# A decode block with a streamed key/value cache: from a framework that unrolls every step to hand-placed waits and hardware loops on two engines

## The chip, the core and the metric

The kernel runs on one core of a Trainium2 chip. The core has five instruction streams: TensorE (PE in the profile, with weight loads as PEld), VectorE (DVE), ScalarE (ACT), GpSimd (POOL) and SyncE (SP), and 16 DMA engines that carry all traffic from and to HBM. The metric is the device time of one execution in microseconds; less is better. The kernel before was timed three times: 1318.71, 1318.73 and 1319.01 us, a median of 1318.73.

## The reference

One token for each of two batch entries goes through attention over a long cache and is gated by a small feed-forward block. All data are float32.

```
xn = layernorm(x)                         # x: [2, 1, 512]
q  = xn @ wq                              # wq: [512, 4096] -> 32 heads of 128
k, v                                      # caches: [2, 8, 32768, 128]; 4 query heads share one
p  = softmax(q . k * 128**-0.5)           # over 32768 tokens
s  = concat(p @ v) @ wo                   # wo: [4096, 512]
g  = silu((relu_gate(xn @ W_gate) * (xn @ W_up)) @ W_down)    # 512 -> 1792 -> 512
out = x + s * g
```

`relu_gate(a)` is `a * (a > 0)`. The two caches are 268 MB each and are read once; the weights are 28 MB.

## The kernel before

**Tiles and steps.** There are 16 groups (batch entry b, key/value head hk), taken as g -> (g % 2, g // 2), with 32768 tokens each. A step handles TK = 8192 tokens of K, a 4 MB load with 64 tokens on each of 128 partitions. A group has NU = 4 steps, so there are NK = 64 steps s, and V runs four steps behind K: step s makes the scores of tile s and, at odd s, multiplies the tiles s - 5 and s - 4 with V. Four more steps (64 to 68) drain this.

**One step.** VectorE turns the K tile in four parts of 128x2048 (`k_transpose`, L336; the last step has its tokens in another order, L339, all others L344) into tiles named `kts`, drawn from a pool of five buffers (`ktpool`, L58). TensorE multiplies them with the query: 16 matmuls on four column groups (`scores`, L350), the first four of them one per part, then eight, and in the last four one per part again. VectorE takes the scores out of PSUM with their maximum (`take_scores`, L366). At a group's end (`tile_maximum`, L381, `maximum`, L387) the maximum over the tiles is turned, spread and negated, and ScalarE takes the exponentials of four tiles. A step later TensorE arranges a tile's weights (`weights`, L411), VectorE transposes them in 32x32 blocks (`take_weights`, L421), and `values` (L424) multiplies with V, 16 matmuls a tile. `sums`, `take_o` and `finish_group` (L440 to L484) divide by the sum, pick the head's own rows and put them, turned by VectorE, into the tile `ots`. At the end `project_near` and `project_far` (L488, L507) multiply `ots` with wo in eight parts, and the result is gated, added to x and stored.

**Loads.** All loads are issued by SyncE in one queue, in the order of the code (`load`, L135, with its DMA at L136). K goes into a ring of two 4 MB buffers: K of step s + 2 is issued when step s has transposed its tile. V comes as 8 MB for two steps into one wide buffer, which wq, the gate and up weights and the down weights use in turn at the start: V of s - 3 and s - 2 is issued at odd s behind K, when the values before it are done. So from step 3 on the queue holds K, K, V (8 MB) for every two steps. At the end come four parts of wo, the last V in halves, and the last four parts of wo, the last one cut in three (`load_late`, L189).

**Order of the work.** The loop at L577 writes one step after another, all unrolled in Python. A tile framework places buffers and derives every semaphore wait from the reads and writes of tiles; `pin` (L559) keeps the order of the code on TensorE and VectorE. In step s the order is: first transposed part; scores of s - 1 taken out; group output; maximum; second and third part; `finish_group`; `weights`; fourth part and `scores(s)`; `take_weights`; `values` at odd s.

## Time and profile before

| | |
|---|---|
| median of three runs | 1318.73 us |
| span of the profiled execution | 1316.7 us |
| instructions in the span | 10568 |
| busy TensorE, matmuls | 894.2 us (68%) |
| busy VectorE | 694.2 us (53%) |
| busy ScalarE | 51.3 us (4%) |
| HBM read | 564.67 MB, 429 GB/s over the span |

The profiled execution has only its span, from its first to its last instruction; what lies around the span is part of the timed 1318.73 us, so that the two stand 2.0 us apart. In the rows of the page, a group of instructions is given as line, engine, operation, tile written <- tiles read, shape and count, then busy time and mean duration, then the idle time of its engine just before them with what ended it. A window row gives a stretch of time, its length, the busy time of PE, PEld, DVE, ACT and POOL with instruction counts, TensorE's granted clock, the mean share of the 16 DMA engines that was busy, and GB/s. The queue rows give a queue, its kind, packets, MB and share of the 16 engines. In SP's timeline a row of two DMAs spans both issues; waits between them are inside.

### The profile page before, as it was taken

How to read it: one execution, taken by the hardware profiler on the slowest of the kernel's cores; microseconds unless marked ns; L12 is line 12 of the kernel's file. 1: busy time of each engine (PE TensorE's matmuls, PEld its weight loads, DVE VectorE, ACT ScalarE, POOL GpSimd, SP SyncE). 2: the span in 40 equal slices, each digit the busy share in tenths (PEclk: the TensorE clock that was granted, in tenths of full speed). 3: DMA queues.
4: the chain of work that ended last, by engine and by line, in shares of the span. 5: the costliest groups of instructions: out<-in, count | busy, mean ns of one | idle time of the engine just before them, and what ended most of it. 6: DMA issues, size and time to landing. Idle time of an engine off the chain costs nothing.

```text
span 1316.7 us, 10568 instructions
## 1 busy us (share of the span) xinstructions
PE 894.2 (68%) x4700; PEld 211.3 (16%) x4700; DVE 694.2 (53%) x627; ACT 51.3 (4%) x133; POOL 0.7 (0%) x6
## 2 busy tenths in 40 slices
PE   3766767576776767766676757766676675676775
PEld 1221111111111111111111111111121111111111
DVE  3676664454665545566454566544466654546611
ACT  0000000000000000000000000000000000000000
POOL 0000000000000000000000000000000000000000
PEclk9777788798788788888888988878878887987798
DMA  9999999999999999999999999999999999999997
GB/s 407 436 429 431 433 450 427 433 424 434 437 438 435 427 432 433 433 430 439 435 442 419 432 432 440 438 433 426 430 436 433 436 436 437 425 432 432 438 423 318
DMA packets 16353, 565.35 MB, mean 429 GB/s; under 512 B 1826, under 2 KB 1842, under 8 KB 2228
## 3 DMA queue, kind: packets, MB, share of 16 engines
q1 hardware_dynamic: 16280, 564.67, 99.3%
q8 instruction: 37, 0.61, 0.2%
q14 instruction: 8, 0.07, 0.0%
q10 hardware_dynamic: 28, 0.01, 0.0%
HBM read 564.67 MB, written 0.00 MB: 429 GB/s over the span
## 4 chain that ended last, share of the span: by engine, by line
DMA 71%; DVE 26%; PE 2%; issue 0%; DVEq 0%; SPq 0%
DMA k<-in_A_k_cache_dram 65%; DVE kts L344 22%; DMA wo_late<-in_A_wo_dram 2%; DMA wo<-in_A_wo_dram 2%; DMA wq<-in_A_wq_dram 2%; DVE sc L371 1%; DVE os L451 1%; PE pq L231 1%; PE s L357 1%; PE pr L399 1%; DVE kts L339 1%; DVE ob L479 0%; DVE mrow L396 0%; DVE nb L403 0%; DVE ots L484 0%
## 5 line engine op out<-in xcount | busy, mean ns | idle before, releaser
L344 DVE STREAM_TRANSPOSE kts<-k 128x2048 f32<-128x2048 f32 x252 | 567.9, 2286 | 482.4 <-DMA k<-in_A_k_cache_dram 482.4
L357 PE MATMUL s<-kts,qt 128*32 128x512 f32 x2048 | 482.4, 714 | 193.5 <-DVE kts L344 191.0
L429 PE MATMUL o_ps<-v,sc 128*16 128x512 f32 x2048 | 256.8, 652 | 81.5 <-DMA v<-in_A_v_cache_dram 81.4
L357 PEld LDWEIGHTS s<-kts,qt 128*32 128x32 f32 x2048 | 91.4, 126 | 585.1 <-DVE kts L344 318.5
L429 PEld LDWEIGHTS o_ps<-v,sc 128*16 128x16 f32 x2048 | 58.1, 103 | 263.4 <-issue 163.6
L407 ACT ACTIVATE sc<-sc,nb 128x512 f32<-128x512 f32 x64 | 45.4, 710 | 1125.1 <-DVE nb L403 1125.1
L413 PE MATMUL pt<-sc,perm 128*128 128x512 f32 x128 | 82.8, 735 | 1.2 <-ACT sc L407 1.1
L371 DVE TENSOR_SCALAR_CACHE_REDUCE sc<-s 128x512 f32<-128x512 f32 x64 | 43.0, 672 | 47.0 <-PE s L357 47.0
L385 PE MATMUL pr<-ident,m 128*1 128x128 f32 x16 | 5.6, 347 | 80.0 <-DVE m L383 80.0
L422 DVE STREAM_TRANSPOSE sc<-pt 128x512 f32<-128x512 f32 x64 | 43.3, 677 | 19.7 <-PE pt L413 19.6
L413 PEld LDWEIGHTS pt<-sc,perm 128*128 128x128 f32 x128 | 23.9, 217 | 57.3 <-issue 44.6
L399 PE MATMUL pr<-negone,mrow 1*128 1x1 f32 x32 | 9.1, 351 | 33.1 <-DVE mrow L396 33.1
L467 PE MATMUL po<-os,heads 128*128 128x512 f32 x32 | 31.3, 1079 | 0.0
L451 DVE SCALAR_TENSOR_TENSOR os<-o_ps,rl,own 128x512 f32<-128x512 f32 x16 | 12.0, 750 | 11.5 <-PE o_ps L429 10.0
L385 PEld LDWEIGHTS pr<-ident,m 128*1 128x1 f32 x16 | 1.3, 79 | 94.7 <-DVE m L383 89.5
L399 PEld LDWEIGHTS pr<-negone,mrow 1*128 1x128 f32 x32 | 7.7, 298 | 37.4 <-DVE mrow L396 37.4
L231 PE MATMUL pq<-wq,xt 128*32 128x512 f32 x64 | 9.3, 744 | 6.0 <-DMA wq<-in_A_wq_dram 6.0
L449 DVE RECIPROCAL rl<-pl 128x1 f32<-128x1 f32 x16 | 2.6, 164 | 17.8 <-PE pl L444 17.8
L407 ACT ACTIVATION_READ_ACCUMULATOR sc<-sc,nb 128x1 f32 x64 | 11.9, 187 | 0.0
L223 PE MATMUL px<-ident,boot 32*128 32x32 f32 x4 | 0.7, 300 | 16.1 <-DVE boot L217 16.1
L339 DVE STREAM_TRANSPOSE kts<-k 128x2048 f32<-128x2048 f32 x4 | 9.0, 2280 | 0.0
L242 DVE COPY qs<-pq 128x512 f32<-128x512 f32 x2 | 1.4, 692 | 14.3 <-PE pq L231 14.3
(79 smaller groups left out, 109.5 us busy)
## 6 DMA issues: line engine op xcount, KB each, us to landing
k<-in_A_k_cache_dram SPq DMA_DIRECT2D x64, 4096.0 KB, 27.0
v<-in_A_v_cache_dram SPq DMA_DIRECT2D x3, 4096.0 KB, 25.6
wo<-in_A_wo_dram SPq DMA_DIRECT2D x4, 1024.0 KB
v<-in_A_v_cache_dram SPq DMA_DIRECT2D x2, 2048.0 KB
wgu<-in_B_W_gate_dram SPq DMA_DIRECT2D x1, 3584.0 KB, 19.6
wgu<-in_B_W_up_dram SPq DMA_DIRECT2D x1, 3584.0 KB
wd<-in_B_W_down_dram SPq DMA_DIRECT2D x1, 3584.0 KB
wo_late<-in_A_wo_dram SPq DMA_DIRECT2D x3, 1024.0 KB, 31.9
```

Source lines behind the costliest of these rows:

```text
L231: nc.tensor.matmul(pq[half][32 * c : 32 * c + 32, :], xn[:, k, :], wqt[:, k, half, c * 512 : (c + 1) * 512], start=(k == 0), stop=(k == NK ...
L339: nc.vector.transpose(part.rearrange("p (h r) e k -> p h (r e k)", h=2), in_halves(KT[t])[:, :, c].rearrange("p h r d -> p h (r d)"),)
L344: nc.vector.transpose(part.rearrange("p r e k -> p (r e k)"), KT[t][:, c].rearrange("p r d -> p (r d)"),)
L357: nc.tensor.matmul(ps[Q * c : Q * c + Q, :], qt[:, b, hk, e, :], kts[c][:, :, e, :], start=(e == 0), stop=(e == 3),)
L371: nc.vector.tensor_scalar(ST[t].rearrange("p r m -> p (r m)"), SPS.pop(t), SCALE, None, op0=ALU.mult, op1=ALU.max, accum_out=MX[g][:, u : ...
L399: nc.tensor.matmul(pr[:, 256:257], mrow.rearrange("o c k h -> o (c k h)"), negone, start=True, stop=True)
L407: nc.scalar.activation(st, st, AF.Exp, bias=nbias, scale=1.0, accum_out=LS[g][:, u : u + 1])
L413: nc.tensor.matmul(PW[t], perm.rearrange("p k c h -> p (k c h)"), ST[t].rearrange("p r m -> p (r m)"), start=True, stop=True,)
L422: nc.vector.transpose(ST[t].rearrange("p r m -> p (r m)"), PW.pop(t))
L429: nc.tensor.matmul(ops[g % 2][a : a + NC * REP, :, :], w[:, r, : NC * REP], v[:, r // 8, :, r % 8, :] if t == NK - 1 else v[:, :, r, :], s ...
L451: nc.vector.scalar_tensor_tensor(OS[g], ops[g % 2], rl, own.unsqueeze(2).to_broadcast([P, NC, DH]), op0=ALU.mult, op1=ALU.mult,)
L467: nc.tensor.matmul(po, heads[:, b].rearrange("p h m -> p (h m)"), o.rearrange("p c d -> p (c d)"), start=(b == 0), stop=(b == B - 1), skip ...
```

## The change

The kernel is written again without the tile framework. What it computes, the loads, their order and the order of steps stay. In detail:

- Buffers are placed by hand. The turned K parts have four fixed tiles, one per part, instead of five in rotation. K has two slots, V the wide buffer, scores, weights, outputs and the small products two PSUM banks each.
- Each operation is recorded with keys that it reads and writes. A class works out which semaphore values it must wait for (one counter for each engine, one semaphore for each load stream) and leaves out what is known already.
- TensorE and VectorE run steps 0 to 7 as straight code, then steps 8 to 63 as a loop of seven passes of eight steps, then steps 64 to 68. In the loop, each awaited value stands in a register that is raised by additions. SyncE, ScalarE and GpSimd stay unrolled.
- All tiles have the order of tokens that only the last step had, so that each pass has the same addresses.
- The turned head outputs, whose place depends on the head, go to a fixed tile on VectorE, and ScalarE copies them to their place. The query of a group is copied by GpSimd into one of two fixed tiles.
- The projection of q is done one half after the other. The frame is a block of engine programs; at the end GpSimd clears the semaphores.

The core of the diff; the class that works out the waits and the set-up code are left out, since they write the same operations in another form:

```diff
+PERIOD = 8
+    def looped(self, engine, first, last):
+        rounds = (last - first) // PERIOD
...
+        for same in zip(*bodies):
+            waits = {}
+            for s in sorted({s for o in same for s in o.waits}):
+                v = max(o.waits[s] - n * stride[s] for n, o in enumerate(same) if s in o.waits)
...
+    def emit(self, engine, eng, sems, loop=None):
...
+        with eng.Fori(0, rounds):
+            for o, waits in body:
+                for s, v in sorted(waits.items(), key=lambda w: w[0] == engine):
+                    if not stride[s]:
+                        eng.wait_ge(sems[s], v)
+                        continue
+                    if v != at[s]:
+                        eng.reg_add(regs[s], regs[s], v - at[s])
+                        at[s] = v
+                    eng.wait_ge(sems[s], regs[s])
+                run(o)
+            for s, r in regs.items():
+                eng.reg_add(r, r, start[s] + stride[s] - at[s])
...
-    ktpool = ctx.enter_context(tc.tile_pool(name="ktpool", bufs=5))
+    kts = [sbuf(f"kts{c}", P, NR * P, align=ALIGN) for c in range(NC)]
...
     def k_transpose(t, c):
-        part = ktpool.tile([P, NR, 4, Q], F32, tag="kt", align_bytes=ALIGN, name=f"kts_{t}_{c}")
-        if t == NK - 1:
...
+        src = kslot[t % 2]
+        dve(
+            lambda e: e.transpose(
+                kts[c].rearrange("p (h n) -> p h n", h=2),
+                in_halves(src)[:, :, c].rearrange("p h r d -> p h (r d)"),
+            ),
+            [f"k{t % 2}"],
+            [f"kts{c}"],
+        )
...
+        for c in range(NC):
+            pe(one(0, c), [f"kts{c}", f"qcur{b}"], [f"s{t % 2}"])
+        pe(chain([one(e, c) for e in (1, 2) for c in range(NC)]), [f"qcur{b}"], [f"s{t % 2}"])
+        for c in range(NC):
+            pe(one(3, c), [f"kts{c}", f"qcur{b}"], [f"s{t % 2}"])
...
+    def take_query(g):
+        b, hk = group(g)
+        pg.op(
+            "POOL" if g >= 2 else "DVE",
+            lambda e: e.tensor_copy(qcur[b], qt[:, b, hk]),
+            ["qt"],
+            [f"qcur{b}"],
+        )
...
-        nc.vector.transpose(ots[:, hk].rearrange("p j m -> p (j m)"), ob)
+        dve(
+            lambda e: e.transpose(ot, ob),
+            ["ob"],
+            ["ot"],
+        )
+        act(
+            lambda e: e.copy(ots[:, hk].rearrange("p j m -> p (j m)"), ot),
+            ["ot"],
+            [f"ots{hk}"],
+        )
...
+    sems = {s: nc.alloc_semaphore(f"sem_{s}") for s in pg.count}
+    with nc.Block(no_gpsimd_drain=True) as block:
...
+        @block.vector
+        def _(e):
+            pg.emit("DVE", e, sems, loop=(PERIOD, NK))
+
+        @block.tensor
+        def _(e):
+            pg.emit("PE", e, sems, loop=(PERIOD, NK))
+
+    nums = sorted(s.num for s in sems.values())
+    nc.gpsimd.sem_clear(range(nums[0], nums[-1] + 1))
```

## The prediction, made before the changed kernel ran

> **What bounds the kernel now.** I read the page's first three parts first, then the busy time by windows, at last the timeline of one pair of steps. Span, load stream and queues:

> ```profile
> span 1316.7 us, 10568 instructions
> PE 894.2 (68%) x4700; PEld 211.3 (16%) x4700; DVE 694.2 (53%) x627; ACT 51.3 (4%) x133; POOL 0.7 (0%) x6
> DMA  9999999999999999999999999999999999999997
> q1 hardware_dynamic: 16280, 564.67, 99.3%
> q8 instruction: 37, 0.61, 0.2%
> q14 instruction: 8, 0.07, 0.0%
> 700.00:1000.00 300.00, 205.61 (x1051) 46.94 (x1050) 159.10 (x138) 11.72 (x32) 0.00 (x0) 0.84 1.00 433
> ```

> The 16 DMA engines carry the loads (q1) for 99.3% of the span; the last two columns of the windows row say share 1.00 at 433 GB/s, with TensorE (PE) busy 205.6 and VectorE (DVE) 159.1 of 300 us. Bytes set the time, and the change moves none of the 564.67 MB. What is left is how the stream starts, how it ends, and what else the same engines carry. That is q8 and q14, packets of instructions: 0.61 MB / 37 = 16 KB and 0.07 MB / 8, some 8 KB. The program has 4700 matmuls and 4700 weight loads; 0.61 MB / 9400 is 65 bytes for each, so q8 brings PE's instructions, 254 to a packet, and an 8 KB packet holds about 128. The end of the stream, by windows (second number from the right: share of 16 engines):

> ```profile
> 1304.00:1305.00 1.00, 1.00 (x12) 0.06 (x4) 0.00 (x0) 0.00 (x0) 0.00 (x0) 0.50 1.00 408
> 1305.00:1306.00 1.00, 1.00 (x8) 0.37 (x8) 0.13 (x1) 0.00 (x0) 0.00 (x0) 0.50 0.70 289
> 1306.00:1308.00 2.00, 2.00 (x10) 0.30 (x2) 0.62 (x1) 0.00 (x0) 0.00 (x0) 0.70 0.57 241
> 1308.00:1309.00 1.00, 1.00 (x10) 0.16 (x8) 0.48 (x1) 0.00 (x0) 0.00 (x0) 1.00 0.55 229
> 1309.00:1310.00 1.00, 0.48 (x8) 0.00 (x0) 0.53 (x2) 0.00 (x0) 0.00 (x0) 1.00 0.50 203
> 1310.00:1311.00 1.00, 0.76 (x8) 0.16 (x8) 0.00 (x0) 0.00 (x0) 0.00 (x0) 1.00 0.45 176
> 1311.00:1312.00 1.00, 0.70 (x20) 0.41 (x16) 0.62 (x1) 0.00 (x0) 0.00 (x0) 1.00 0.24 94
> 1312.00:1312.50 0.50, 0.50 (x27) 0.38 (x16) 0.07 (x1) 0.00 (x0) 0.00 (x0) 1.00 0.08 29
> ```

> Share times 16 is the number of engines still loading: 16 until 1305, then 9, 8 from 1309, 4 from 1311, none after 1312.2. Seven engines finish at about 1305.3 (in that second 0.30 x 16 = 4.8 engine-us are missing, 0.7 for each of seven), one at 1308.8, four at 1310.8, four at 1312.2. All have equal bytes, so nine were held up: by 3.5, 5.5 and 6.9 us. I read this as the instruction packets: dealt in turn to eight engines, 36 packets make five on four of them and four on the other four (the 37th may come after the data). 6.9 / 5 = 1.38 and 5.5 / 4 = 1.38: both steps give the same **toll of 1.38 us per 16 KB packet**. The ninth engine, 3.5 us late, would hold VectorE's packets (627 instructions and some 60 waits, 5 to 6 packets: 0.58 each; between 3.5 / 8 = 0.44 and half of 1.38). The chain behind the last byte:

> ```profile
> 1302.96 2.85 PE L429 MATMUL o_ps<-v,sc 128*16 128x512 f32 x16 [2.07 <-DMA v<-in_A_v_cache_dram]
> 1309.25 0.31 DVE L484 STREAM_TRANSPOSE ots<-ob 128x128 f32<-128x128 f32 x1
> 1311.61 0.64 PE L516 MATMUL py<-wo_late,ots 128*32 128x128 f32 x16 [0.30 <-DMA wo_late<-in_A_wo_dram]
> 1312.37 0.82 PE L516 MATMUL py<-wo_late,ots 128*32 128x128 f32 x16
> 1313.90 0.65 SPq L624 DMA_DIRECT2D out_dram<-gy  x1
> ```

> Each load counts as landed with its slowest engine, and the last rows of wo end the kernel: what the worst engine loses to packets, the kernel loses.

> **The change, part by part.** *The loops.* Rows for one period of eight steps:

> ```profile
> L357 PE MATMUL s<-kts,qt 128*32 128x512 f32 x2048 | 482.4, 714 | 193.5 <-DVE kts L344 191.0 <-DVE kts L339 2.5
> L429 PE MATMUL o_ps<-v,sc 128*16 128x512 f32 x2048 | 256.8, 652 | 81.5 <-DMA v<-in_A_v_cache_dram 81.4
> L413 PE MATMUL pt<-sc,perm 128*128 128x512 f32 x128 | 82.8, 735 | 1.2 <-ACT sc L407 1.1
> ```

> By 64 steps that is 32 + 32 + 2 matmuls a step and as many weight loads, 132; eight steps 1056, two group ends 14 each: 1084. From `emit` I count some 57 waits with as many register additions and ten instructions of the loop, so about 1210, 4.8 packets. A matmul of the code is two matmuls and two weight loads in the trace (2048 at L357 for 64 x 16), so the straight steps 0 to 7 are 512 for scores, 16 and 256 for weights and values, 184 for q, 352 for the gated block, ten for a group end and some 60 waits: 1390 (5.5 packets). Steps 64 to 68 are 16 and 256, 192 for wo and some 26 more: 490 (1.9). If a pass finds its instructions still in place, PE loads 5.5 + 4.8 + 1.9, with one ahead at the loop's end 13 packets in place of 37: at most two on an engine, 2.8 us in place of 6.9. VectorE's body is 72 instructions (nine per step with group ends), 51 waits, 51 additions and eight of the loop: 182, 1.4 packets; all told some 430 instead of 690, 3 to 4 packets, 2.3 us on its engine, less than 2.8. Gain: 6.9 - 2.8 = **4.1 us**. If each pass loads its body anew, PE loads 5.5 + 7 x 4.8 + 1.9 = 41, up to 55 when every pass adds a cut packet and one past the end: six or seven on the worst engine, 8.3 to 9.7 us, a loss of 1.4 to 2.8. VectorE then loads 12 + 7 to 14, 19 to 26 packets, all on one engine: 19 x 0.58 = 11.0 to 15.1 us, a loss of 4.1 to 8.2. Nothing in this trace loops, so the trace can't say which; both ends stay in the range. I take the first: the staircase fits packets that go to eight places in turn, and 1210 instructions fill five or six of eight.

> [...]

> *The waits and edges of the loop.* A pass's jump may stall an engine, by how much nothing here shows; what hides it is in one pair of steps:

> ```profile
> 642.13 2.31 DVE L344 STREAM_TRANSPOSE kts<-k 128x2048 f32<-128x2048 f32 x1 [16.86 <-DMA k<-in_A_k_cache_dram]
> 652.84 5.32 PE L357 MATMUL s<-kts,qt 128*32 128x512 f32 x32
> 653.83 12.03 SPq L136 DMA_DIRECT2D k<-in_A_k_cache_dram  x2
> 654.32 2.27 DVE L344 STREAM_TRANSPOSE kts<-k 128x2048 f32<-128x2048 f32 x1
> 671.06 7.06 PE L429 MATMUL o_ps<-v,sc 128*16 128x512 f32 x64 [0.23 <-DMA v<-in_A_v_cache_dram]
> 678.18 0.33 SPq L136 DMA_DIRECT2D v<-in_A_v_cache_dram  x1
> 680.78 2.31 DVE L344 STREAM_TRANSPOSE kts<-k 128x2048 f32<-128x2048 f32 x1 [14.69 <-DMA k<-in_A_k_cache_dram]
> k<-in_A_k_cache_dram SPq DMA_DIRECT2D x64, 4096.0 KB, 27.0
> ```

> A pass ends behind an odd step, where VectorE sits idle for 14.7 us until K lands: a stall up to that costs nothing.

> *Four transposed tiles in place of five.* The first transpose of a step now waits until the scores of the step before have read that tile, ten of the last 13 matmuls. In the odd step above it starts at 654.32 while scores run 652.84 to 658.16; it would start near 657, 2.7 us later, and with it the three transposes, the scores and the issue of K, which leaves SyncE (SP) behind them. A K load takes 27.0 us from issue to landing, its own 4.19 MB at 433 GB/s 9.7 of them: 17 us of other loads lie ahead of it, on the engines ahead of the rest some 5 less. 2.7 comes out of that. The V load waits for the values, and these for V's landing at 671, later than the moved scores: nothing. The tightest place lies in the straight steps:

> ```profile
> 79.45 13.19 SPq L136 DMA_DIRECT2D k<-in_A_k_cache_dram  x2
> 79.48 3.62 PE L357 MATMUL s<-kts,qt 128*32 128x512 f32 x26 [0.61 <-DVE kts L344]
> 79.58 2.31 DVE L344 STREAM_TRANSPOSE kts<-k 128x2048 f32<-128x2048 f32 x1 [0.15 <-DMA k<-in_A_k_cache_dram]
> 0.74 0.40 SPq L136 DMA_DIRECT2D wq<-in_A_wq_dram  x1
> ```

> The second K issue of the first row, K of step 5, ends at 92.6 and begins some 0.3 before. Ahead of it lie wq 8.39 MB, five K of 4.19 and three weights of 3.67, 40.4 MB, or 93.2 us of a stream that was issued at 0.74: gone 94.0 us in, with the same way from issue to first byte. The transpose waits until 79.48 + 3.62 x 10 / 13 = 82.3 instead of 79.58, so the issue moves from 92.3 to 95.0, and an engine without lag runs dry for 1 us, once; an engine with a packet behind it, 1.4 us late, does not. I take nothing and keep 0 to 1.

> *The rest.*

> ```profile
> L344 DVE STREAM_TRANSPOSE kts<-k 128x2048 f32<-128x2048 f32 x252 | 567.9, 2286 | 482.4 <-DMA k<-in_A_k_cache_dram 482.4
> L339 DVE STREAM_TRANSPOSE kts<-k 128x2048 f32<-128x2048 f32 x4 | 9.0, 2280 | 0.0
> L333 ACT ACTIVATE gy<-ps_d 128x128 f32<-128x128 f32 x1 | 0.3, 277 | 76.8 <-PE ps_d L326 76.8
> SPq L136 <- DMA v<-in_A_v_cache_dram: 207.0, 33, 9.3
> ```

> One order of tokens keeps shapes and counts: L339, which has that order now, takes 2280 ns, L344 2286; nothing. ScalarE's copy of the turned head outputs is on the path only in the last group: ots at 1309.56, needed at 1311.61, 2.05 us of cover for about 0.3 (the activation at L333 is nearest, 277 ns) and a hop. If that cover went, 0.4 us of loss. GpSimd's copy of a group's query has four steps to finish. SyncE still issues wq first, 0.74 us in, and its waits for earlier loads that share a semaphore (207.0 us in 33 waits for V) go; the stream is full, so nothing. The frame around the program stays a barrier at either end, within 0.4 us both ways.

> Sum: 4.1 us less. The profiled execution has a span of 1316.7; the median is 1318.73, 2.0 beside it, taken as unchanged. 1318.7 - 4.1 = **1314.6 us**, a profile span of 1312.6.

> **The rivals.** [...]

> *Half the gain, or none*: VectorE's body stays and PE's does not, 1320.1 to 1321.5; or a part of PE's is reloaded, about 30 packets, four on an engine, 5.5 in place of 6.9: 1317.3. Either is within 0.2%.

> *The stream runs dry*: if waits on registers delay the odd steps by over some 10 us, each us more is paid in each of some 28 pairs in the loop; 1 us gives 1347. Against it: the idle 14.7 us, and PE's 205.6 of 300.

> *The loop does nothing*, should it be unrolled again when built: 37 packets as now, 1318.7. I put it with the second.

> **How the numbers follow.** Forecast 0.50; half or none 0.14; loaded anew 0.30; dry 0.06. 0.2% is 2.6 us, about what a measurement of this kernel can tell from no change. So faster 0.50, same 0.14, slower 0.36. Forecast alone: one to three packets on the worst engine, 1313.2 to 1316.0. The range reaches from there through the second case and the larger part of the third, to 1325.0; above it lie the end of the third case (0.08) and the dry one.

> **What would show it.** Right: q8 falls from 37 packets to 12 to 15, the staircase ends within 3 us of its first step, windows in the loop stay at 433 GB/s. [...] A DMA share under 0.98 in windows of 300 us is the dry one. The prediction is wrong at its root if the staircase stays while q8 shrinks: then the packets were not what held the nine engines up.

## The result and the profile after

The changed kernel takes 1315.38 us, the median of nine runs (1314.80 to 1317.09), beside 1318.87 us for the kernel before on the same chip: a ratio of 0.9977, 95% interval 0.9968 to 0.9985. It is 3.5 us faster; 1314.6 us was forecast. The profiled execution is the slowest of the nine, 1317.09 us with a span of 1315.2, so its last microseconds show more than the median has.

The page of the kernel after, first its span, then the load queue and the two queues of instruction packets (packets, MB, share):

```profile
span 1315.2 us, 11033 instructions
...
q1 hardware_dynamic: 16280, 564.67, 99.5%
q8 instruction: 11, 0.18, 0.0%
q14 instruction: 4, 0.03, 0.0%
```

The load is the same to the byte. TensorE's packets (q8) fell from 37 to 11, the packets of 8 KB (q14) from 8 to 4. The same queues of the kernel after, by stretches: 0 to 350 us (TensorE's first pass of the loop ends at about 330), 350 to 1260, and 1260 to 1312:

```profile
q8 instruction: 9, 0.15, 0.1%
...
q1 hardware_dynamic: 10172, 394.33, 100.2%
q14 instruction: 2, 0.02, 0.0%
...
q8 instruction: 2, 0.03, 0.2%
```

Nine of TensorE's packets come while it goes through the straight steps and the first pass, two when it leaves the loop. In the 910 us between, six more passes, there is no row for q8 at all: a pass finds its instructions in place. The two packets of q14 in that stretch move at about 424 and 955 us. One moves at 420 to 424 and one at 952 to 959 us in every kernel of the experiments too, whether VectorE loops or not; so these two belong to an engine that stays unrolled. q14 is not VectorE's alone: of its four packets here the other two, at about 68 and 267 us, are taken as VectorE's.

Windows of the kernel after, one in the loop and then the end of the stream (the last two columns are the DMA share and GB/s):

```profile
700.00:1000.00 300.00, 208.75 (x1054) 51.38 (x1054) 164.13 (x140) 12.32 (x34) 1.17 (x4) 0.82 1.00 434
1304.00:1305.00 1.00, 1.00 (x9) 0.16 (x9) 0.24 (x1) 0.00 (x0) 0.00 (x0) 1.00 0.98 410
1305.00:1306.00 1.00, 1.00 (x2) 0.22 (x2) 0.00 (x0) 0.00 (x0) 0.00 (x0) 1.00 0.96 389
1306.00:1307.00 1.00, 0.67 (x9) 0.16 (x8) 0.88 (x2) 0.00 (x0) 0.00 (x0) 1.00 0.90 356
1307.00:1308.00 1.00, 0.45 (x7) 0.00 (x0) 0.12 (x1) 0.30 (x1) 0.00 (x0) 1.00 0.48 186
1308.00:1309.00 1.00, 0.12 (x4) 0.12 (x8) 0.00 (x0) 0.00 (x0) 0.00 (x0) 1.00 0.12 47
1309.00:1310.00 1.00, 0.94 (x8) 0.03 (x5) 0.00 (x0) 0.00 (x0) 0.00 (x0) 1.00 0.06 25
1310.00:1311.00 1.00, 0.80 (x24) 0.65 (x28) 0.69 (x1) 0.00 (x0) 0.00 (x0) 1.00 0.06 25
```

The loop runs at 434 GB/s, so its waits cost the stream nothing. Two things differ at the end. The long plateau of eight engines at 0.55 is gone: most engines finish between 1306.5 and 1309. But the first step comes later than before: share 0.96 from 1305 to 1306, where it was 0.70. So something holds up even the engines that finish first by more than a microsecond, and in this execution one engine alone (0.06 x 16 = 1) loads on to nearly 1311.

Where that first loss lies is seen in step 3. The timeline of the kernel after, first the K issues of SyncE, then the first transpose of step 3 and the scores that it waits for (the bracket is idle time and what ended it):

```profile
79.41 16.00 SPq L237 DMA_DIRECT2D k<-in_A_k_cache_dram  x2
79.44 3.62 PE L240 MATMUL s<-kts,qcur 128*32 128x512 f32 x26 [0.57 <-DVE kts L648]
82.35 2.31 DVE L648 STREAM_TRANSPOSE kts<-k 128x2048 f32<-128x2048 f32 x1 [2.97 <-PE s L240]
```

The transpose waits for the scores of the step before, 82.35 instead of 79.58, and the second K issue of the first row, that of step 5, ends at 95.4 instead of 92.6: 2.8 us later, where 2.7 was worked out. What the stream made of it stands in the windows from 90 to 210 us, of the kernel before and then of the kernel after:

```profile
90.00:210.00 120.00, 82.36 (x497) 21.91 (x490) 64.92 (x55) 7.42 (x18) 0.00 (x0) 0.82 1.00 433
```

```profile
90.00:210.00 120.00, 80.92 (x485) 22.28 (x481) 67.70 (x56) 7.51 (x18) 0.58 (x2) 0.85 1.00 428
```

5 GB/s less over 120 us are 0.6 MB, or 1.4 us of a stream of 433 GB/s. That was taken as nothing, with 0 to 1 us kept.

The end of the chain, in the timeline of the kernel after:

```profile
1307.16 0.30 ACT L834 COPY ots<-ot 128x128 f32<-128x128 f32 x1 [39.95 <-DVE ot L829]
...
1310.20 0.64 PE L240 MATMUL s<-k,ots 128*32 128x128 f32 x16 [0.26 <-DMA k<-in_A_wo_dram]
...
1312.59 0.64 SPq L237 DMA_DIRECT2D out_dram<-gy  x1
```

ScalarE's copy ends at 1307.5 and is needed at 1310.2, where the matmul waits for wo: the copy is covered by 2.7 us. The kernel still ends with the slowest engine's last bytes of wo.

### The profile page after: what moved, and what is told of

It is laid out like the page before. It is cut to its first block, busy times and chain, and to the rows that moved or that the text cites. A ratio compares the mean times of both kernels' runs of the same rounds, so it can differ in the third digit from the quotient of the medians.

```text
span 1315.2 us, 11033 instructions
## 1 busy us (share of the span) xinstructions
PE 903.2 (69%) x4700; PEld 221.5 (17%) x4700; DVE 695.4 (53%) x627; ACT 53.8 (4%) x141; POOL 4.8 (0%) x20
## 2 busy tenths in 40 slices
DMA  9999999999999999999999999999999999999997
## 3 DMA queue, kind: packets, MB, share of 16 engines
q1 hardware_dynamic: 16280, 564.67, 99.5%
HBM read 564.67 MB, written 0.00 MB: 429 GB/s over the span
## 4 chain that ended last, share of the span: by engine, by line
DMA 68%; DVE 19%; issue 7%; PE 5%; DVEq 0%; SPq 0%
DMA k<-in_A_k_cache_dram 61%; DVE kts L648 15%; DMA k<-in_A_wo_dram 3%; DMA w<-in_A_v_cache_dram 2%; DMA w<-in_A_wq_dram 2%; PE m_ps L240 2%; DVE st L675 2%; PE o L240 1%; PE s L240 1%; PE pt L240 1%; DVE ob L820 0%; DVE mrow L715 0%; DVE mr L705 0%; DVEq L150 0%; DVE m L691 0%
## 5 line engine op out<-in xcount | busy, mean ns | idle before, releaser
L240 PE MATMUL s<-kts,qcur 128*32 128x512 f32 x2048 | 510.0, 734 | 215.9 <-DVE kts L648 215.7
L240 PE MATMUL o<-w,st 128*16 128x512 f32 x1984 | 236.7, 613 | 39.6 <-DMA w<-in_A_v_cache_dram 39.6
L240 PEld LDWEIGHTS s<-kts,qcur 128*32 128x32 f32 x2048 | 92.6, 128 | 636.0 <-DVE kts L648 462.3
L240 PEld LDWEIGHTS o<-w,st 128*16 128x16 f32 x1984 | 66.4, 99 | 188.1 <-issue 127.7
L730 ACT ACTIVATE st<-st,nb 128x512 f32<-128x512 f32 x64 | 45.4, 710 | 1121.7 <-DVE nb L726 1121.7
L240 PE MATMUL pt<-st,perm 128*128 128x512 f32 x128 | 83.4, 740 | 1.1 <-ACT st L730 1.1
L746 DVE STREAM_TRANSPOSE st<-pt 128x512 f32<-128x512 f32 x64 | 43.3, 677 | 17.8 <-PE pt L240 17.7
L675 DVE TENSOR_SCALAR_CACHE_REDUCE st<-s 128x512 f32<-128x512 f32 x64 | 41.8, 653 | 3.1 <-PE s L240 3.1
L240 PEld LDWEIGHTS pt<-st,perm 128*128 128x128 f32 x128 | 23.9, 217 | 57.3 <-issue 45.4
L240 PE MATMUL m_ps<-os,heads 128*128 128x512 f32 x32 | 31.3, 1079 | 0.0
## 6 DMA issues: line engine op xcount, KB each, us to landing
k<-in_A_k_cache_dram SPq DMA_DIRECT2D x64, 4096.0 KB, 26.1
k<-in_A_v_cache_dram SPq DMA_DIRECT2D x2, 4096.0 KB, 27.2
w<-in_A_v_cache_dram SPq DMA_DIRECT2D x1, 4096.0 KB, 33.6
```

Of the source, the lines that this page charges most:

```text
L240: return lambda e: e.matmul(out_, lhs, rhs, start=start, stop=stop, skip_group_check=True)
L675: lambda e: e.tensor_scalar(st[t % NST], ps_s[t % 2], SCALE, None, op0=ALU.mult, op1=ALU.max, accum_out=mx[g % 2][:, u : u + 1],),
L730: lambda e, t=t, u=u: e.activation(st[t], st[t], AF.Exp, bias=nb[i], scale=1.0, accum_out=ls[i][:, u : u + 1]),
L746: lambda e: e.transpose(st[t % NST], ps_p[t % 2]),
```

## Experiments

**The theory**: instruction packets take time from the load engines, so the loops gain what the worst engine no longer loses, and the late K issue of step 3 takes part of it back. **Rivals**: the gain comes from something else in the new version (token order, frame, ScalarE's copy, loads that no longer wait for shared semaphores); or only one of the two loops matters; or the late issue is harmless, as forecast, and the missing microsecond is chance.

Times are medians, with the lowest and highest run; the kernel before stood at 1318.70 to 1318.77 us beside them.

### Which loop gains, with the four tiles of the change

**e2_no_loop**: the changed kernel with steps 8 to 63 written out on both engines. **e3_pe_loop** and **e4_dve_loop** keep one loop each. The edit of the first; each of the others has half of it:

```diff
-            pg.emit("DVE", e, sems, loop=(PERIOD, NK))
+            pg.emit("DVE", e, sems)
...
-            pg.emit("PE", e, sems, loop=(PERIOD, NK))
+            pg.emit("PE", e, sems)
```

Expected:

> The changed kernel with both loops written out again, all else kept. Theory (the gain is instruction packets that the loops save): 37 packets of 16 KB and 7 to 9 of 8 KB, the staircase of before at the end with steps of 1.4 us up to 7 us, and 1318.7 plus up to 1 us for the late K issue: 1318.5 to 1320. Rival (the gain is in the hand-placed waits and the frame without the tile framework): 1315 to 1316 with 37 packets.

> The changed kernel with TensorE's loop kept and VectorE's steps written out. Theory: 11 packets of 16 KB as in the changed kernel, 5 to 8 packets of 8 KB that meet on one DMA engine at 0.58 us each, which then ends 3 to 4 us behind the first; 1315.0 to 1316.5, at most 1 us over the changed kernel. Rival (each loop is worth half): 1317.

> The changed kernel with VectorE's loop kept and TensorE's steps written out. Theory: 37 packets of 16 KB, eight engines late by four or five tolls of 1.38 us, 1318.5 to 1320, as without any loop. Rival (each loop is worth half): 1317.

Measured: e2 1320.81 us (1319.95 to 1322.43), ratio 1.0017 (1.0008 to 1.0026); e3 1318.26 (1316.60 to 1319.29), ratio 0.9996 (0.9987 to 1.0005); e4 1320.63 (1318.94 to 1321.85), ratio 1.0015 (1.0006 to 1.0024). The instruction packets of e2, from its page:

```profile
q8 instruction: 36, 0.59, 0.2%
q14 instruction: 8, 0.07, 0.0%
```

Without its loops the new version has the packets of the kernel before and is even 2.1 us slower: the rest of the rewriting gains nothing, and something in it costs 2 us. From e2 to the changed kernel the loops bring 5.4 us. The median of e2 is 0.8 us above the range expected, that of e4 0.6. VectorE's loop alone (e4) brings next to nothing: TensorE still has 36 packets, as the theory has it. TensorE's loop alone (e3) brings 2.6 us, and its runs scatter over 2.7 us; its median lies beyond the range expected (to 1316.5) and beyond the rival's 1317. The profiled run of e3 (1316.63 us) is near the lowest of its eleven; in its windows a single engine is late even so:

```profile
1308.00:1309.00 1.00, 0.54 (x8) 0.16 (x8) 0.00 (x0) 0.00 (x0) 0.00 (x0) 1.00 0.07 29
1309.00:1310.00 1.00, 0.75 (x17) 0.25 (x13) 0.40 (x1) 0.00 (x0) 0.00 (x0) 1.00 0.06 25
```

0.06 x 16 is one engine again. The sizes with four tiles are blurred by that scatter, so the next runs take the late issue away first.

### The same with five tiles

**e1_five_tiles**: the changed kernel with a fifth tile, so that the first part of a step alternates between two and needn't wait for the scores before. **e7_five_no_loop** is this with both loops written out, **e8_five_pe_loop** with VectorE's written out.

```diff
-    kts = [sbuf(f"kts{c}", P, NR * P, align=ALIGN) for c in range(NC)]
+    kts = [sbuf(f"kts{c}", P, NR * P, align=ALIGN) for c in range(NC + 1)]
...
+    def part_of(t, c):
+        return NC if c == 0 and t % 2 else c
```

Expected:

> The changed kernel with a fifth turned K tile: the first part of even and odd steps alternates between two tiles, so the first transpose of a step no longer waits for the scores of the step before. Theory (the engines that finish first lost about 1 us when K of step 5 was issued at 95.1, and one engine lost 2.8 us in the same moment): K of step 5 is issued near 92.3, no engine runs dry, the first DMA engines finish about 1 us earlier than in the changed kernel (1306.8 us into the span), the last ones at most 3 us behind the first, median 1313.5 to 1314.6 us, and the scatter of the runs of 2.3 us shrinks under 1. Rival (late issue and scatter have nothing to do with each other, or the odd steps' waits cost nothing anywhere): 1314.8 to 1317, as the changed kernel.

> Five turned K tiles, both loops written out. Theory (what the loops save is all of the gain, and the frame, the one order of tokens and ScalarE's copy are worth nothing): 36 or 37 packets of 16 KB, the staircase of before, the time of before, 1318.2 to 1319.2 us, with a scatter under 1 us, since the late K issue is gone. Rival (the hand-placed waits save something of their own): 1316 to 1317.5.

> Five turned K tiles, TensorE's loop kept, VectorE's steps written out. Theory (VectorE's packets meet on one DMA engine at 0.58 us each): 8 packets of 8 KB instead of 4, one engine alone ends last, about 4 us behind the first, 1 us behind the one that ends last with both loops: 1314.6 to 1315.6 us against 1314.1. Rival (VectorE's loop is worth the 2.9 us between the medians with four tiles, 1318.26 and 1315.38): 1317.

Measured: e1 1314.10 us (1313.94 to 1314.14), ratio 0.9965 (0.9951 to 0.9978); e7 1318.75 (1318.16 to 1319.73), ratio 0.9999 (0.9990 to 1.0008); e8 1315.26 (1315.04 to 1315.39), ratio 0.9973 (0.9962 to 0.9984). All nine runs of the changed kernel lie above all five of e1, the lowest by 0.7 us. Of e1, the K issues of SyncE and the transpose in step 3, then the windows:

```profile
79.38 13.40 SPq L237 DMA_DIRECT2D k<-in_A_k_cache_dram  x2
...
79.72 2.31 DVE L652 STREAM_TRANSPOSE kts<-k 128x2048 f32<-128x2048 f32 x1 [0.37 <-DMA k<-in_A_k_cache_dram]
```

```profile
90.00:210.00 120.00, 80.94 (x500) 21.32 (x494) 65.06 (x55) 7.51 (x18) 0.59 (x2) 0.87 1.00 433
...
1305.00:1306.00 1.00, 0.10 (x4) 0.10 (x8) 0.00 (x0) 0.00 (x0) 0.00 (x0) 1.00 0.67 264
1306.00:1307.00 1.00, 0.96 (x8) 0.05 (x8) 0.00 (x0) 0.00 (x0) 0.00 (x0) 1.00 0.41 160
1307.00:1308.00 1.00, 0.78 (x24) 0.63 (x28) 0.69 (x1) 0.00 (x0) 0.00 (x0) 1.00 0.17 64
1308.00:1309.00 1.00, 0.84 (x24) 0.31 (x16) 0.10 (x1) 0.00 (x0) 0.00 (x0) 1.00 0.00 0
```

The transpose waits for K again, the K issue ends 2.6 us earlier (92.8), the stretch from 90 to 210 us is back at 433 GB/s, the first engines end at 1305 as before the change, and the last one some 3 us behind them. Written out, the same kernel (e7) has the staircase of the kernel before, and its time:

```profile
1305.00:1306.00 1.00, 1.00 (x12) 0.31 (x8) 0.00 (x0) 0.00 (x0) 0.00 (x0) 0.50 0.65 270
...
1310.00:1311.00 1.00, 0.46 (x6) 0.16 (x8) 0.00 (x0) 0.21 (x1) 0.00 (x0) 1.00 0.44 176
1311.00:1312.00 1.00, 0.73 (x13) 0.16 (x9) 0.33 (x1) 0.00 (x0) 0.00 (x0) 1.00 0.25 98
```

So with five tiles the rewriting is worth 0.0 us (1318.75 beside 1318.74 us of the kernel before; the interval of the ratio leaves some 1.2 us either way), and the loops 1318.75 - 1314.10 = **4.65 us**: TensorE's 3.49 (e7 to e8), VectorE's 1.16 on top (e8 to e1). What is left in e8 is one engine, by the theory the one that carries VectorE's packets. Its page and windows:

```profile
q8 instruction: 11, 0.18, 0.0%
q14 instruction: 7, 0.06, 0.0%
```

```profile
1307.00:1308.00 1.00, 0.94 (x8) 0.16 (x8) 0.00 (x0) 0.00 (x0) 0.00 (x0) 1.00 0.23 88
1308.00:1309.00 1.00, 0.73 (x24) 0.47 (x24) 0.69 (x1) 0.00 (x0) 0.00 (x0) 1.00 0.07 29
```

After 1308 one engine (0.07 x 16 = 1.1) still loads, to about 1309.2, some 4.2 us behind the first ones. If all seven packets of 8 KB lay on it, that is 0.6 us for each; but two of the seven move at 420 and 954 us and are not VectorE's, and with the other five alone it is 0.8. The rows do not name the engine that carries a packet, so the toll of a packet of 8 KB stays between these. The late issue shows again between e3 and e8, which differ by the fifth tile alone: 3.0 us. The scatter of e7, 1.6 us, was expected below 1; it stays unexplained.

### The late K issue by itself

Three kernels for the other half. **e6_gate_later** keeps four tiles and moves the gated block's part of step 3 behind the scores, which makes room ahead of the K issue. **e9_late_k** has five tiles and does VectorE's copies for the gated block seven times instead of two (the result of each repeats the one before), which makes the issue of K as late as in the changed kernel with no wait for scores. **e10_after_again** is the changed kernel itself, for a second trace. Edits of e6 and e9:

```diff
-        for f, a in taken.get(s, []):
-            f(*a)
...
+        for f, a in taken.get(s, []):
+            f(*a)
```

```diff
-        for i in range(2):
+        for i in (0, 1, 0, 1, 0, 1, 0):
```

Expected:

> The changed kernel with its four turned K tiles; in step 3 alone VectorE's five operations of the gated block and TensorE's down projection move behind the transposes and scores. The odd steps keep their wait of 2.97 us. Theory (the loss against five tiles lies in the one late K issue of step 3): K of step 5 is issued near 92, no engine runs dry, 1313.9 to 1314.6 us with a scatter under 1 us. Rival (the waits in the odd steps cost it): 1315.4 with the scatter of 2 us.

> Five turned K tiles and both loops, the fastest version so far (1314.1 us, K of step 5 issued at 92.45); VectorE copies the gated block's two products out of PSUM seven times instead of twice in step 3, about 2.8 us more, so that K of step 5 is issued near 95.2 as in the changed kernel. Nothing else waits longer. Theory (one late K issue makes all of the difference between four and five tiles): the first DMA engines end about 1 us later, and 1315 to 1316 us with a scatter of 1 to 2.5 us. Rival (the waits in the odd steps of the loop made it): 1314.1 with a scatter of 0.2 us.

> The changed kernel again, for a second profile. Theory: K of step 5 issued at 94 to 95.5, first engines done 1306 to 1307, a last engine 2.4 to 4.6 us behind, by chance; 1314.8 to 1317.1 us. Rival (the first profile was a stray one): all engines within 3 us at the end in every run and no late K issue.

Measured: e6 1314.80 us (1313.96 to 1315.48), ratio 0.9970 (0.9957 to 0.9982); e9 1316.44 (1314.80 to 1316.79), ratio 0.9979 (0.9970 to 0.9989); e10 1315.58 (1315.00 to 1317.46), ratio 0.9977 (0.9967 to 0.9987). Of e9, the row of the K issues, then the window from 90 to 210 us and two of the end:

```profile
79.44 15.97 SPq L237 DMA_DIRECT2D k<-in_A_k_cache_dram  x2
```

```profile
90.00:210.00 120.00, 82.65 (x478) 21.44 (x473) 67.80 (x56) 7.51 (x18) 0.58 (x2) 0.83 1.00 426
...
1306.00:1307.00 1.00, 0.81 (x8) 0.00 (x0) 0.45 (x2) 0.30 (x1) 0.00 (x0) 1.00 0.88 352
...
1309.00:1310.00 1.00, 0.73 (x20) 0.41 (x16) 0.63 (x1) 0.00 (x0) 0.00 (x0) 1.00 0.16 61
```

Of e10, the same:

```profile
79.59 17.00 SPq L237 DMA_DIRECT2D k<-in_A_k_cache_dram  x2
```

```profile
90.00:210.00 120.00, 85.20 (x510) 22.99 (x506) 68.89 (x56) 7.51 (x18) 0.59 (x2) 0.82 0.99 425
...
1308.00:1309.00 1.00, 0.75 (x24) 0.44 (x22) 0.69 (x1) 0.00 (x0) 0.00 (x0) 1.00 0.48 182
1309.00:1310.00 1.00, 0.98 (x27) 0.50 (x24) 0.00 (x0) 0.00 (x0) 0.00 (x0) 1.00 0.02 6
```

e9 has the five tiles and all the loops of e1. Its K issue ends at 95.4 instead of 92.8, the stretch falls to 426 GB/s (7 GB/s over 120 us, 0.84 MB or 1.9 us), and its median is 2.3 us above that of e1: the late issue alone costs that much (the median is 0.4 us above the range expected). e10 issues K still later, 96.6, with the scores before it slower this time; 8 GB/s are lost (2.2 us), and the whole staircase comes later, with hardly an engine behind the rest: none but one loads after 1309, where a last engine 2.4 to 4.6 us behind was expected. e6 was expected to issue K at about the time of e1; in its profile it was 94.1, because the scores that the transpose waits for took 5.67 us instead of 3.62, at a lower granted clock (0.63 from 79 to 85 us, 1.00 in the changed kernel). So e6 undoes the delay in part, and its median lies 0.7 us above e1 and 0.6 below the changed kernel, 0.2 above the range expected; its runs scatter over 1.5 us, where under 1 was expected. In e6 the stretch runs at 429 GB/s, a loss of 1.1 us. So the late issue is no chance: in four profiles of three kernels (the changed kernel twice, e9, e6) it took 1.1 to 2.2 us from the stretch, and 0.7 to 2.3 from the median beside e1. How much of it reaches the end varies: e10 loses more in the stretch than e9, and less in the median.

It costs as much where the loops are written out and the lags at the end are long: between e7 and e2, which differ by the fifth tile alone, 2.1 us. The reason can be seen in what had moved by then. The queues of e2 from 0 to 94 us:

```profile
q8 instruction: 2, 0.03, 0.1%
q14 instruction: 1, 0.01, 0.0%
```

In the kernel before, in the changed kernel and in e1, e3, e7 and e8 these two counts are the same. The loops begin at step 8, so by 94 us no version has more lag than another, and three packets can have held up three of the 16 engines at most.

### How long a body may be

**e5_five_body16**: five tiles, and loops of three passes of 16 steps (steps 8 to 55), the rest straight. TensorE's body is twice as long.

```diff
-            pg.emit("PE", e, sems, loop=(PERIOD, NK))
+            pg.emit("PE", e, sems, loop=(PERIOD, NK - PERIOD, 2 * PERIOD))
```

Expected:

> Five turned K tiles; loops of three passes of 16 steps (8 to 55), steps 56 to 63 written out. TensorE's body is then some 2270 instructions, 8.9 packets of 16 KB, VectorE's some 240, 1.9 packets of 8 KB. Theory (a pass finds its instructions in place only while the body fits into eight packets of 16 KB): each pass loads anew, 36 to 40 packets of 16 KB, 1318 to 1319.5 us. Rival (a loop keeps its instructions at any size, or the place is larger): 20 or 21 packets, three or four on an engine, 1314.5 to 1316. The packets of 8 KB tell the same of VectorE: 5 or 6 if its body stays, 8 or more if not.

Measured: 1319.61 us (1319.54 to 1320.53), ratio 1.0008 (0.9999 to 1.0017). The queues of e5, the page's rows first, then q8 for 0 to 350, 350 to 1260 and 1260 to 1312 us:

```profile
q8 instruction: 42, 0.69, 0.2%
q14 instruction: 5, 0.04, 0.0%
...
q8 instruction: 10, 0.16, 0.2%
...
q8 instruction: 30, 0.49, 0.2%
...
q8 instruction: 2, 0.03, 0.2%
```

Where the short body loads nothing between 350 and 1260 us, the long one loads 30 packets. A pass takes some 310 us here, so the first one ends near 490. Were the body kept, 4 packets of the first pass and 5 of the straight steps at the end would lie in this stretch; the 21 others are two passes of 8.9 packets, with cut ones at their edges: each pass loads anew. That is 42 packets where 36 to 40 were expected, and a median 0.1 us above the range. VectorE's body, twice as long too, stays: of the five packets of q14 the last two come at 462 us, where its first pass ends, and at 959, which is the one of another engine. So a body that each pass loads anew, put at 0.30 in the forecast, is real for a longer one: it costs TensorE's loop all it brings, and 0.9 us more than no loop at all (e7).

## Why the prediction was right

**The packets' toll and the loops: right.** The steps on record hold one after another: the load engines carry the packets, a pass finds its instructions in place, and what the worst engine no longer lags the kernel gains. That all engines have equal bytes stands in no row of the trace before; e10, whose share goes from 0.96 (1306 to 1307 us) over 0.48 (1308 to 1309) to 0.02 (1309 to 1310), fits it within some 2 us. That TensorE's packets go to eight engines in turn was read from the staircase; the times that the packets themselves take in the trace before fit it, as they repeat every eight packets (0.95, 0.88, 0.89, 0.94, 0.93, 0.93, 0.97, 0.97 us, then 0.95, 0.88, 0.89, 0.94 and so on). The toll of 1.38 us is more than these 0.9; what the rest is, no run shows. The toll has now been varied: with five tiles, 11 packets of TensorE give 1314.10 us, 36 give 1318.75 and 42 give 1319.61 (with 4, 7 and 5 packets of 8 KB). From 36 to 42 that is 0.14 us a packet; over eight engines 1.38 / 8 = 0.17 was implied. The 0.86 us behind the 0.14 are small beside e7's scatter of 1.6, so this is a rough agreement. VectorE's toll of 0.58 us per packet, all on one engine, was neither confirmed nor refuted: e8 gives 0.6 or 0.8, by how many packets lay there. The gain of the loops alone was put at 4.1 us and is 4.65; the half microsecond between them is within the scatter of e7.

**The counts: near, with one step wrong.** Waits were counted as instructions of their own, 57 in TensorE's body and 51 in VectorE's. Most aren't: e2, straight throughout, has 36 packets of 16 KB, 0.59 MB, which is 63 bytes for each of the 9400 matmuls and weight loads alone; some 500 waits as instructions would be two packets more. In e2's trace TensorE has no semaphore instruction in steps 8 to 63, and VectorE has ten in every eight steps. What the loops add can be read off the spans' instruction counts of e2, e3 and e4, in this order:

```profile
span 1318.6 us, 10428 instructions
```

```profile
span 1314.8 us, 10769 instructions
```

```profile
span 1318.1 us, 10692 instructions
```

TensorE's loop adds 341, five ahead of it and 48 in each of seven passes; VectorE's 264, five ahead and 37 in each (44 of the loop less seven of the ten waits). So the bodies are 1084 + 48 = 1132 instructions (4.4 packets) and 72 + 10 + 37 = 119 (under one packet of 128), as many as the changed kernel's trace has in a pass, where 1210 and 182 stood. Hence 11 packets instead of 13.

**Whether a pass reloads: right, and now bounded.** A body of 4.4 packets stays, with no packet of TensorE's in 910 us of the changed kernel's loop; one of 8.9 is loaded anew in each pass, 30 packets in the same stretch (e5). Eight places of 16 KB would do that, and so would any number from five to eight: the eight of the forecast and of what was expected of e5 was the author's estimate, from the eight engines of the staircase, and no run tried a length between. The range's end at 1325.0 came from a VectorE that loads its body in each pass, at a loss of 4.1 to 8.2 us: no run shows that, and e5, where TensorE's body is loaded anew, takes 1319.61. The jump itself costs nothing that can be seen: the loop keeps 434 GB/s.

**Four tiles: the step that failed.** When the late K issue would come was on record to a tenth of a microsecond (wait 2.7 us, issue of K of step 5 from 92.3 to 95.0, measured 95.1 for its start). So was its effect on an engine without lag, dry for 1 us, once: from 90 to 100 us the changed kernel loads at 382 GB/s where e1 loads at 431, a loss of 1.1 us. The term that was mis-sized is its price, taken as nothing with 0 to 1 kept. Measured, between kernels without and with the late issue: 1.3 us between e1 and the changed kernel, 2.3 between e1 and e9, 2.1 between e7 and e2, 3.0 between e8 and e3. The reason for taking nothing was that an engine late by a packet would not run dry. But the lags that the staircase shows at 1305 us were mostly not there at 95 us: by 94 us two packets of TensorE and one of q14 had moved, with loops or without, so at least 13 of 16 engines had no such lag. An engine without a lag runs dry, and so the staircase moves as a whole: e2's last two steps, shares of 0.19 and 0.08, stand from 1312 to 1314 us, e7's, 0.25 and 0.08, from 1311 to 1313. Why it costs up to 3 us, when the stretch from 90 to 210 us loses 0.8 to 2.2, and why it brings the scatter, stays open. In the changed kernel's profile a single engine loads on to 1311; which engine it is and why was not found.

**The total.** 4.65 us of the loops less 1.3 of the late issue are 3.35; measured 3.5 beside the kernel before. The forecast of 4.1 less nothing came near partly by luck, because two errors offset each other: the gain was 0.55 too small, the cost 1.3.

**The rest: right at nothing, as a sum.** e7 has everything but the loops and the four tiles and takes 1318.75 us beside 1318.74. Token order, ScalarE's copy, GpSimd's copy, SyncE's dropped waits and the frame together cost nothing within some 1.2 us; no run takes them one by one.

**The marks set beforehand.** q8 in 12 to 15: 11 came, one less. Windows in the loop at 433 GB/s (434): right. A staircase that ends within 3 us of its first step: right for e10 and nearly for e1, not for the profiled run of the changed kernel, whose lone engine ends over 4 us behind.

**The best version** is e1: loops on both engines and five tiles, 1314.10 us.

## What to carry to other kernels

When loads fill all the time, look at what else the same queues carry: here instruction packets left single engines up to 7 us behind the rest, and a loop whose body is loaded once gave most of it back, while a body twice as long gave back nothing. Before rolling up steps, count a body's instructions in packets, and look at the traffic of one pass in the middle of the loop to see that it stays. A lag covers a late issue only on the engines that have it at that moment: here the lags grew over the whole kernel and covered little of a late issue at its start, with loops or without.
